# Batch 0's queries and keys stay float32 through TensorE in a one-core attention and two-MLP kernel

## The chip, the cores and the metric

The program runs on one core of one Trainium2 chip. The metric is device time in microseconds (us), from the first to the last instruction of the slowest core with the little that lies around them. Lower is better.

## The reference

Inputs are q, k, v of shape (4, 8, 576, 64) in float32, a decay f of shape (4, 8, 576), two weight matrices of a first MLP (512 x 2048 and 2048 x 512) and two of a second (512 x 1024 and 1024 x 512); the weights come as 8-byte floats.

```python
scores = 0.125 * q @ k.T + cum[:, None] - cum[None, :]   # cum = cumsum(log f), causal mask
x = softmax(scores) @ v                                  # 4 batches, 8 heads, 576 rows
h = x @ w_in;  g = h * tanh(softplus(h));  y = g @ w_out # 2304 tokens
h2 = y @ w2_in; solu = h2 * softmax(h2)
out = layernorm(solu) * g_ln @ w2_out
```

## The kernel before

**Halves.** TensorE is given float16. A float32 operand is scaled by a power of two from a bound of it, and split in a high and a low half (`split`, L181); a product of two such operands takes three float16 matmuls, or one where both halves lie side by side in the 128 rows of the contraction, as in the scores.

**Attention.** A batch has five row tiles of 128 rows (the last has 64). For batch 0 `load_raw` fetches a chunk of 128 rows of all 8 heads (256 KB), `stats` takes sums of squares of k on ScalarE, `scales` turns their maximum over all five k chunks into powers of two, and only then `split_k` and `split_q` make the halves (q's low half on GpSimd). `turn` transposes them with eight float16 matmuls against an identity and two ScalarE copies out of PSUM for a chunk; in the later batches a DMA transpose does it. Then VectorE copies the key's high half (L408) and the query's high half (L439) to the tiles of the second matmul. `scores` issues for every head a matmul over 128 contraction rows (L474), a second one over 67 rows (L475) that carries the missing product and the three rows of the decay, and on the diagonal a mask (L479). The decay rows come from a scan on VectorE, go out to DRAM (`dd`) and return by a DMA (L409).

`step_r` takes the row maximum on VectorE (L525) and the exponential on ScalarE (L527). `step_h` makes the halves of the probabilities, high by ScalarE (L565), low by GpSimd (L566), and has a DMA transpose them (L571). `step_pv` multiplies them with the halves of v, three matmuls for each head and chunk (L597 to L599), after `split_v` has scaled v by a bound over all five chunks. `fin` divides by the row sums and sends the result through a DMA transpose (L624) to `xT`, the first MLP's input.

**First MLP.** Blocks j of 256 tokens; `up` (L842) has 16 slices of 12 matmuls, `down` (L886) 16 slices of 6. Block j = 0 is exactly row tiles 0 and 1 of batch 0. It is worked weight group by weight group while the weights still arrive: 16 parts of 1 MB (W1 and W2 in four groups each), loaded into two buffers (L114), turned from 8-byte floats to float32 in three VectorE instructions (L124, L126, L128), bounded through TensorE (L147) and split; the first eight parts are split through TensorE with a float32 matmul against a diagonal (L191). Block j = 1 needs all of them.

**Order.** A planner (`Order.pin`, near the end) lays all instructions out with costs of its own, and pins the order on every engine. So each engine runs its list in order, and one instruction that waits holds all behind it. SP issues all DMAs.

Of the kernel before, what the change touches and what calls it, by code (L numbers as in the profile page):

```python
# [10 lines left out]
F32 = mybir.dt.float32  # L11
# [195 lines left out]
def emit(tc, q, k, v, f, w_in, w_out, w2_in, w2_out, g_ln, out):  # L207
# [7 lines left out]
    make_identity(nc, ident)  # L215
    ident16 = const.tile([P, P], F16, name="ident16")
    nc.vector.tensor_copy(ident16, ident)
    maskd = const.tile([P, P], BF16, name="maskd")
# [6 lines left out]
    nc.gpsimd.memset(ones, 1.0)  # L225
    c_k1 = const.tile([P, 1], F32, name="c_k1")
    nc.vector.memset(c_k1, 0.2)

    us2 = const.tile([P, NTT], F32, name="us2")
    ivt = const.tile([P, B], F32, name="ivt")  # L230
    iv = [ivt[:, b:b + 1] for b in range(B)]
    usc1 = [const.tile([P, 4], F32, name=f"usc1_{b}") for b in range(B)]
    wpt = const.tile([P, 4], F32, name="wpt")
    wps = [wpt[:, g:g + 1] for g in range(4)]
    kb = [const.tile([P, 1], F32, name=f"kb{b}") for b in range(B)]
    ipwo = const.tile([P, 1], F32, name="ipwo")
    kbz = const.tile([P, 1], F32, name="kbz")
    rho = const.tile([P, 4], F32, name="rho")
    ths = const.tile([P, 4], F32, name="ths")
    rcol = const.tile([P, 2], F32, name="rcol")  # L240

# [35 lines left out]
    ktr = att.tile([P, NKT, 2 * H, P], F16, name="ktr")  # L277
    kn = [att.tile([P, H * P], F16, name=f"kn{i}") for i in range(KNB)]
# [70 lines left out]
    def scales(b, which):  # L349

        j0 = "kv".index(which[0])
        n = len(which)
        t = att.tile([P, 6, 2], F32, tag="sct", name=f"sct{which}_{b}", bufs=1)
        x = [t[:, i, :n] for i in range(6)]
        nc.vector.tensor_reduce(x[0], sc["st", b][:, j0:j0 + n], axis=AX.X, op=ALU.max)
        src = across(x[0], x[1])
        nc.vector.tensor_scalar(x[1], src, 2.0 ** -40, None, op0=ALU.max)
        root2(nc, x[4], x[1])
        nc.vector.reciprocal(x[5], x[4])
        for i, nm in enumerate(which):  # L360
            pw, ip = t[:, 4, i:i + 1], t[:, 5, i:i + 1]
            if nm == "k":
                u = att.tile([P, 2], F32, tag="scu", name=f"scu_{b}", bufs=2)
                c = 64.0
                nc.vector.tensor_scalar(u[:, 0:1], pw, 0.125 / c, None, op0=ALU.mult)
                nc.vector.tensor_scalar(u[:, 1:2], ip, c, None, op0=ALU.mult)
                sc["q", b], sc["k", b] = u[:, 0:1], u[:, 1:2]
            else:
                u = att.tile([P, 1], F32, tag="scv", name=f"scv_{b}", bufs=2)
                nc.vector.tensor_scalar(u, ip, 2.0 ** 14, None, op0=ALU.mult)  # L370
                nc.vector.tensor_scalar(iv[b], pw, 2.0 ** -14, None, op0=ALU.mult)
                sc["v", b] = u

# [7 lines left out]

    def turn(dst, src, r0, r1_, nm):

        n = dst.shape[1]
        for x in range(0, n, 4):
            t = psh.tile([P, 2, TB], F32, tag="h", name=f"h_{nm}_{x}").rearrange("p g (y s) -> p (g y) s", s=P)
            for y in range(4):
                nc.tensor.matmul(
                    t[:, y, r0:r1_], src[r0:r1_, (x + y) * P:(x + y + 1) * P], ident16[r0:r1_, r0:r1_],
                    start=True, stop=True)  # L390
            nc.scalar.copy(dst[:, x:x + 4, r0:r1_], t[:, :, r0:r1_])

    def split_k(b, c):
        r0, r1_, t0 = rows_of(b, c)
        n = r1_ - r0
        t = kn[cnt["kn"] % KNB]
        cnt["kn"] += 1
# [5 lines left out]
        kt[b, c] = kc  # L403
        if b == 0:
            turn(kc[:, :H], t, r0, r1_, f"k{c}")
        else:
            nc.sync.dma_start_transpose(out=kc[:, :H, r0:r1_], in_=t[r0:r1_, :H * P])
        nc.vector.tensor_copy(kc[:64, H:, r0:r1_], kc[64:, :H, r0:r1_])  # L408
# [17 lines left out]
    def split_q(b, c):  # L426
        r0, r1_, t0 = rows_of(b, c)
        t = attd.tile([P, H, P], F16, tag="qn", name=f"qn_{b}_{c}", bufs=1)
# [3 lines left out]
        qa = attd.tile([P, H, P], F16, tag="qa", name=f"qa_{b}_{c}", bufs=2)  # L432
        if b == 0:
            turn(qa, t.rearrange("p h d -> p (h d)"), r0, r1_, f"q{c}")
        else:
            nc.sync.dma_start_transpose(out=qa[:, :, r0:r1_], in_=t[r0:r1_].rearrange("p h d -> p (h d)"))
# [20 lines left out]
    def scores(o, b, i, h, cs):  # L457
# [3 lines left out]
        for c0, c1 in runs(b, cs):  # L461
# [4 lines left out]
            d = o[:, w + a0 - o0(b, cs):w + 128 * (n - 1) + a1 - o0(b, cs)]  # L466
            k = ktr[:, s:s + n]
            if n > 1:
                d = d.rearrange("p (c s) -> p c s", s=P)
                k1, k2 = k[:, :, h], k[:67, :, H + h]  # L470
            else:
                k1, k2 = k[:, 0, h, a0:a1], k[:67, 0, H + h, a0:a1]
            diag = c1 == i + 1
            nc.tensor.matmul(d, qa[:, h, r0:r1_], k1, start=True, stop=False)  # L474
            nc.tensor.matmul(d, qb_[:67, h, r0:r1_], k2, start=False, stop=not diag)  # L475
# [68 lines left out]
    def step_h(b, i, hs):  # L544
        m, pt = pend.pop(("p", b, i, hs))
        n = len(hs) * (i + 1)
        h0, o = hs[0], 0
        if n == i + 1 and h0 % 2:
# [26 lines left out]
    def step_pv(b, i, hs):  # L575
# [25 lines left out]
    def fin(b, i):  # L601
# [9 lines left out]
        x32 = attd.tile([P, DM], F32, tag="x32", name=f"x32_{b}_{i}", bufs=1)  # L611
        nc.vector.tensor_tensor(
            hd(x32[:m]), hd(acc[:m]), rr[:m].unsqueeze(2).to_broadcast([m, H, D]), op=ALU.mult)
        xh = attd.tile([P, 2, DM], F16, tag="xh", name=f"xh_{b}_{i}", bufs=1)
# [32 lines left out]
    wlo = [rp0]  # L647
    ident32 = rp0.tile([P, P], F32, name="ident32")
    nc.vector.tensor_copy(ident32, ident)
    minus = rp0.tile([P, P], F16, name="minus")  # L650
# [51 lines left out]
    def ahead(b, i, h):  # L702
# [10 lines left out]
        if nb < B:  # L713
# [4 lines left out]
            if h == (LD + 2 if ni else 4):  # L718
                if nb or ni > 1:
                    split_k(nb, ni)  # L720
                    split_q(nb, ni)
                split_v(nb, ni)

# [63 lines left out]

    for c in range(NCH):
        load_raw(0, c, "k", pool0(c))
    for c in range(2):  # L790
        load_raw(0, c, "q", pool0(c))
    for n in range(WPF):
        W1.load(n)
    load_raw(0, 0, "v", pool0(0))
    for c in range(NCH):
        stats(0, c, "k")
    scales(0, "k")
    for c in range(2):
# [6 lines left out]
    for c in range(NCH):
        stats(0, c, "v")
    scales(0, "v")
    split_v(0, 0)
    for n in range(n0 + LAG):
# [10 lines left out]
    def segs(j):  # L820
        r = []
        t = j * TB
        while t < (j + 1) * TB:
            b = t // S
            e = min((b + 1) * S, (j + 1) * TB)
            r.append((b, t - j * TB, e - j * TB))
            t = e
# [76 lines left out]
    def evac(j, t):  # L904
# [12 lines left out]
        for p0 in (0, 64):  # L917
# [145 lines left out]
class Order:  # L1063
# [46 lines left out]
    def trace(self):  # L1110
# [6 lines left out]
        for i in list(self.tc.nc.cur_bb.bb.instructions):  # L1117
# [580 lines left out]
```

## Time and profile before

| | |
|---|---|
| median of 3 runs | 781.82 us (780.08 to 782.59) |
| profiled execution | 780.57 us, of which span 778.8 us |
| TensorE (PE) busy | 722.9 us, 93% of the span |
| VectorE (DVE) / ScalarE (ACT) / GpSimd (POOL) busy | 564.6 / 576.1 / 393.5 us |
| chain that ended last | PE 74%, DVE 8%, ACT 7%, DMA 5% |

PE's busy time is near the span, but not evenly: the last 579 us have almost no idle PE, the first 200 us have most of it. So the table is to be read by stages.

### The profile page before, as it was taken

To read this page: it belongs to the slowest core of one execution; us is meant where nothing else is said; L and a number is where in the kernel's file an instruction comes from. 1 tells how busy PE (TensorE), PEld (TensorE's weight loads), DVE (VectorE), ACT (ScalarE), POOL (GpSimd) and SP (SyncE) were. 2 spreads that over 40 slices of the span, in tenths; PEclk is the share of its full clock that TensorE was granted. 3 is DMA by queue.
4 is the path that set the end of the run, shared out by engine and by line. 5 is a ranking of instruction groups with operands and counts; after the bars stand their busy time and mean duration, and the time that the engine had idled before them with its cause. 6 is when DMAs were issued, how large, how long until landed. Compare 5 with 4: busy or idle time off the path is not lost.

```text
span 778.8 us, 16034 instructions
## 1 busy us (share of the span) xinstructions
PE 722.9 (93%) x5950; PEld 458.9 (59%) x5950; DVE 564.6 (72%) x1140; ACT 576.1 (74%) x1286; POOL 393.5 (51%) x319
## 2 busy tenths in 40 slices
PE   1679889779999999999999999999999999999997
PEld 0444655557666677777777776765565554444443
DVE  5999997878789877789778645878785545375560
ACT  4787898988999999999999868995874553133331
POOL 2245355777776576786788742393472221122221
PEclk9999998899999999999999999999999999999999
DMA  8989986879999898889999446603215325345423
GB/s 242 247 238 268 258 158 120 154 152 190 164 183 169 170 197 185 164 147 173 159 177 162 82 96 163 216 29 122 44 54 107 68 55 104 86 95 121 99 65 94
DMA packets 295226, 112.49 MB, mean 144 GB/s; under 512 B 280492, under 2 KB 281260, under 8 KB 295148
## 3 DMA queue, kind: packets, MB, share of 16 engines
q1 hardware_dynamic: 295148, 111.48, 67.2%
q8 instruction: 46, 0.75, 0.4%
q14 instruction: 32, 0.26, 0.1%
HBM read 46.59 MB, written 9.55 MB: 72 GB/s over the span
## 4 chain that ended last, share of the span: by engine, by line
PE 74%; DVE 8%; ACT 7%; DMA 5%; issue 2%; POOL 2%; SPq 1%; ACTq 0%; POOLq 0%; DVEq 0%
PE x L886 21%; PE h L842 20%; PE h L1606 12%; PE o L1646 11%; PE sp L474 2%; PE sp L475 2%; DMA wi_r<-in_moe_w_in_dram 2%; PE pv L597 2%; ACT p L527 1%; PE pv L599 1%; PE pv L598 1%; DMA pT<-ph 1%; DVE nm L525 1%; DVE wout L126 1%; DVE wout L128 1%
## 5 line engine op out<-in xcount | busy, mean ns | idle before, releaser
L886 PE MATMUL x<-wout,gt 128*128 128x512 f16 x864 | 215.2, 381 | 3.7 <-POOL gt L869 3.7
L842 PE MATMUL h<-xT,win 128*128 128x256 f16 x1728 | 214.0, 275 | 2.3 <-ACT th L855 1.7
L842 PEld LDWEIGHTS <-win 128*128 128x128 f16 x1728 | 167.7, 99 | 42.2 <-issue 4.1
L566 POOL TENSOR_TENSOR ph<-p,ph 128x512 f16<-128x512 f32 (+4 forms) x120 | 155.9, 1306 | 70.6 <-ACT ph L565 64.2
L869 POOL TENSOR_TENSOR gt<-th,gt 128x512 f16<-128x512 f32 x72 | 93.6, 1301 | 97.6 <-ACT gt L868 95.5
L886 PEld LDWEIGHTS <-gt 128*128 128x128 f16 x864 | 80.1, 98 | 74.4 <-POOL gt L869 5.2
L1634 POOL TENSOR_TENSOR z<-sl,z 128x1024 f16<-128x1024 f32 x18 | 38.3, 2126 | 118.8 <-DVE s2c L1613 57.5
L1606 PE MATMUL h<-w,x2T 128*128 128x512 f16 x432 | 96.0, 379 | 0.0
L1646 PE MATMUL o<-wo,zT 128*128 128x512 f16 x432 | 95.5, 379 | 0.4 <-DMA zT<-z 0.4
L863 DVE SCALAR_TENSOR_TENSOR th<-ta,th 128x512 f32<-128x512 f32 x72 | 63.9, 887 | 20.2 <-ACT ta L862 18.2
L1646 PEld LDWEIGHTS <-zT 128*128 128x128 f16 x432 | 42.2, 98 | 51.7 <-DMA zT<-z 0.9
L1606 PEld LDWEIGHTS <-x2T 128*128 128x128 f16 x432 | 42.3, 98 | 50.1
L854 ACT ACTIVATE ta<-h,usc 128x512 f32<-128x512 f32 (+3 forms) x96 | 54.8, 582 | 21.5 <-PE h L842 18.8
L527 ACT ACTIVATE p<-sp,nm 64x64 f32<-64x64 f32 (+7 forms) x128 | 62.3, 492 | 7.7 <-DVE nm L525 5.1
L474 PE MATMUL sp<-ktr,qa 128*128 128x64 f16 (+6 forms) x304 | 56.9, 249 | 11.3 <-ACT p L527 7.1
L475 PE MATMUL sp<-ktr,qb 67*128 67x64 f16 (+6 forms) x304 | 61.2, 250 | 2.8 <-DVE qb L439 2.8
L1617 ACT ACTIVATE e<-h,s2c 128x1024 f32<-128x1024 f32 x18 | 21.7, 1203 | 55.7 <-DVE s2c L1615 51.6
L859 DVE TENSOR_SCALAR ta<-ta 128x512 f32<-128x512 f32 x72 | 49.0, 683 | 17.8 <-ACT ta L854 17.5
L525 DVE TENSOR_REDUCE nm<-sp 128x1 f32<-128x320 f32 (+7 forms) x88 | 48.7, 561 | 15.9 <-PE sp L479 9.3
L597 PE MATMUL pv<-vt,pT 128*128 128x64 f16 (+2 forms) x480 | 53.8, 197 | 2.2 <-DMA pT<-ph 2.2
L868 ACT CAST gt<-th 128x512 f16<-128x512 f32 x72 | 44.6, 619 | 13.1 <-DVE th L863 12.7
L598 PE MATMUL pv<-vt,pT 128*128 128x64 f16 (+2 forms) x480 | 53.4, 196 | 0.5 <-DVE vt L197 0.5
(250 smaller groups left out, 1447.5 us busy)
## 6 DMA issues: line engine op xcount, KB each, us to landing
wi_r<-in_moe_w_in_dram SPq DMA_DIRECT2D x8, 1024.0 KB
wo_r<-in_moe_w_out_dram SPq DMA_DIRECT2D x8, 1024.0 KB
x2d<-x2h SPq DMA_DIRECT2D x18, 256.0 KB
out_dram<-ro SPq DMA_DIRECT2D x18, 256.0 KB
w2i_r<-in_moe_w_in_dram SPq DMA_DIRECT2D x4, 1024.0 KB
w2o_r<-in_moe_w_out_dram SPq DMA_DIRECT2D x4, 1024.0 KB
rawk<-in_k_dram SPq DMA_DIRECT2D x13, 256.0 KB
rawv<-in_v_dram SPq DMA_DIRECT2D x13, 256.0 KB
```

The costliest lines, as they stand in the source:

```text
L474: nc.tensor.matmul(d, qa[:, h, r0:r1_], k1, start=True, stop=False)
L475: nc.tensor.matmul(d, qb_[:67, h, r0:r1_], k2, start=False, stop=not diag)
L527: nc.scalar.activation(pv[:m, g * (i + 1) * P + off:g * (i + 1) * P + end], s3[:, g, off:end], AF.Exp, bias=nm[:m, g:g + 1], accum_out=rs[ ...
L566: nc.gpsimd.tensor_tensor(p4[:, :, 1], pv3, p4[:, :, 0], op=ALU.subtract)
L597: nc.tensor.matmul(o, pT[a0:a1, k, :m], vh, start=(c == 0), stop=False)
L598: nc.tensor.matmul(o, pT[a0:a1, k, :m], vl, start=False, stop=False)
L842: nc.tensor.matmul(ph, win[:, (fi // 4) * NC1 + c, col:col + P], x[:, lx * NC1 + c, :], start=(m == 0), stop=(m == 3 * NC1 - 1))
L863: nc.vector.scalar_tensor_tensor(th, ta, 2.5, th, op0=ALU.subtract, op1=ALU.mult)
L869: nc.gpsimd.tensor_tensor(gt[:, 1], th, gt[:, 0], op=ALU.subtract)
L886: nc.tensor.matmul(o, gt[:, lg, n % 2, t * P:(t + 1) * P], wout[:, fi, lw * 512:(lw + 1) * 512], start=(first and m == 0), stop=(last and ...
L1606: nc.tensor.matmul(h[:, half * 512:(half + 1) * 512], x[:, lx * NC1 + c, :], self.w2[:, half * NC1 + c, lw * 512:(lw + 1) * 512], start=(n ...
L1646: nc.tensor.matmul(o, zT[:, lz * NF2 + c, :], self.wo[:, c, lw * 512:(lw + 1) * 512], start=(n == 0), stop=(n == 3 * NF2 - 1))
```

## The change

In batch 0, q and k are no longer bounded, scaled or split. `turn` transposes the raw float32 chunk with four float32 matmuls; k goes by one ScalarE copy to `kt32`, a float32 view of the space that `ktr` has for halves, and q by two ScalarE copies (each of 64 partitions, scaled by 0.125) to a tile that holds two heads with zeros around them, so that the first score matmul is float32 over 128 rows. The second one stays and brings only the decay (zeros elsewhere, set by GpSimd at the start). For row tiles 0 and 1 the probabilities too are transposed by float32 matmuls and copied by ScalarE, and multiplied with raw v, one float32 matmul for a head and chunk; a bound over the first two v chunks serves block j = 0 alone. The halves of v are made later, for tiles 2 to 4. The q tiles of batch 0 lie in the space of `kn` and of the later batches' query tiles. The first loads become k, q, k, q, v, v of chunks 0 and 1, then the weights, then the rest. The planner's cost of a float32 matmul changes.

```diff
+    kt32 = ktr.rearrange("p k h s -> p (k h s)").bitcast(F32).rearrange("p (k x s) -> p k x s", k=NKT, s=P)
+    knt = att.tile([P, KNB, H * P], F16, name="knt")
+    kn = [knt[:, i] for i in range(KNB)]
+    qat = att.tile([P, 2, H * P], F16, name="qat")
+    q32 = [t.rearrange("p k s -> p (k s)").bitcast(F32).rearrange("p (x y s) -> p x y s", y=2, s=P) for t in (knt, qat)]
+    nc.gpsimd.memset(qb[0][:64].rearrange("p h s -> p (h s)").bitcast(F32), 0.0)
+    for t in q32:
+        nc.gpsimd.memset(t[64:, :, 0], 0.0)
+        nc.gpsimd.memset(t[:64, :, 1], 0.0)
+    for c in range(NCH):
+        nc.gpsimd.memset(kt32[:64, c, 4:], 0.0)
...
+    def turn(dst, src, r0, r1_, nm, scale=1.0):
+        t = psh.tile([P, 2, TB], F32, tag="h", name=f"h_{nm}").rearrange("p g (y s) -> p (g y) s", s=P)
+        n = src.shape[-1] // P
+        for y in range(n):
+            nc.tensor.matmul(
+                t[:, y, r0:r1_], src[r0:r1_, y * P:(y + 1) * P], ident32[r0:r1_, r0:r1_], start=True, stop=True)
+        if type(dst) is list:
+            for y, d in enumerate(dst):
+                nc.scalar.activation(d[:, :, r0:r1_], t[64 * y:64 * y + 64, :, r0:r1_], AF.Copy, scale=scale)
+            return
+        nc.scalar.copy(dst[:, :n, r0:r1_], t[:, :n, r0:r1_])
...
+        if b == 0:          # split_k
+            x = (b * NCH + c) % NKT
+            turn(kt32[:, x, :4], raw["k", b, c], r0, r1_, f"k{c}")
...
+        if b == 0:          # split_q
+            qa = q32[c % 2]
+            turn([qa[:64, :, 0], qa[64:, :, 1]], raw["q", b, c], r0, r1_, f"q{c}", 0.125)
+            qt[b, c] = qa, qb[0]
+            return
...
+                q1, k1 = qa[:, h // 2, h % 2, r0:r1_], kt32[:, s:s + n, h // 2]     # scores, batch 0
+            nc.tensor.matmul(d, q1, k1, start=True, stop=False)
...
+        if b == 0 and i < 2:     # step_h
+            turn(p4, pt.rearrange("p c s -> p (c s)")[:, :n * P], 0, m, f"p{i}_{hs[0]}")
...
+        if b == 0 and i < 2:     # step_pv
+                    nc.tensor.matmul(
+                        acc[:m, h * D:(h + 1) * D], pT[:, g * (i + 1) + c, :m], raw["v", b, c][:, h * D:(h + 1) * D],
+                        start=(c == 0), stop=(c == i))
...
+    for c in range(2):
+        load_raw(0, c, "kq", pool0(c))
+    for c in range(2):
+        load_raw(0, c, "v", pool0(c))
     for n in range(WPF):
         W1.load(n)
-    for c in range(NCH):
-        stats(0, c, "k")
-    scales(0, "k")
```

## Rows read from the trace of the kernel before

**Rows 1.** Busy time by stretch: each engine (instructions), granted clock, DMA share, GB/s.

```profile
0.00:25.00 25.00, 5.87 (x44) 4.55 (x45) 15.75 (x33) 13.50 (x27) 6.84 (x15) 1.00 0.80 215
25.00:50.00 25.00, 17.15 (x111) 12.84 (x111) 24.80 (x53) 17.95 (x55) 8.07 (x6) 1.00 1.05 286
50.00:110.00 60.00, 51.55 (x461) 32.71 (x460) 56.46 (x114) 52.84 (x107) 26.91 (x19) 0.97 0.92 229
110.00:200.00 90.00, 77.65 (x824) 53.74 (x823) 75.39 (x135) 80.89 (x204) 61.71 (x53) 0.91 0.84 159
200.00:778.80 578.80, 570.71 (x4518) 355.01 (x4514) 392.19 (x810) 410.94 (x897) 289.96 (x228) 1.00 0.60 124
```

**Rows 2.** The chain of waits, first 200 us: start, length, what.

```profile
84.71 2.56 PE h L842 x12
...
120.49 6.58 DMA pT<-ph
```

**Rows 3.** Timeline of PE, at the lower and then the higher level.

```profile
25.70 0.31 PE L474 MATMUL sp<-ktr,qa 128*128 128x128 f16 x1
...
27.98 0.31 PE L474 MATMUL sp<-ktr,qa 128*128 128x128 f16 x1
28.08 0.31 PE L475 MATMUL sp<-ktr,qb 67*128 67x128 f16 x1
...
59.57 1.10 PE L191 MATMUL h_lo<-wout,wo_dg 128*128 128x512 f32 x2
60.52 0.38 PE L192 MATMUL h_lo<-wout,minus 128*128 128x512 f16 x1
60.73 1.02 PE L191 MATMUL h_lo<-wout,wo_dg 128*128 128x512 f32 x2
...
70.45 0.19 PE L598 MATMUL pv<-vt,pT 128*128 128x64 f16 x1
70.48 0.19 PE L599 MATMUL pv<-vt,pT 128*128 128x64 f16 x1
...
76.05 0.33 PE L346 MATMUL sp<-wi_b,ones 128*128 128x1 f32 x2
76.24 0.62 PE L147 MATMUL sp<-wout 128*128 128x128 bf16 x8
```

**Rows 4.** Groups of DVE up to 110 us: line, count, busy us, mean ns.

```profile
L126 DVE SCALAR_TENSOR_TENSOR wout<-wo_r,wout 128x1024 int32<-128x1024 int32 x8 | 12.5, 1565 | 0.1
...
L408 DVE COPY ktr<-ktr 64x1024 f16<-64x1024 f16 (+1 forms) x5 | 2.8, 567 | 0.2
L197 DVE SCALAR_TENSOR_TENSOR kn<-wout,scu,kn 128x512 f16<-128x512 f32 x3 | 2.2, 742 | 1.3 <-ACT kn L196 1.3
L439 DVE COPY qb<-qa 64x1024 f16<-64x1024 f16 (+1 forms) x5 | 1.9, 388 | 0.1
```

**Rows 5.** Groups of ACT up to 110 us.

```profile
L391 ACT CAST qa<-h_q 128x512 f16<-128x512 f32 (+1 forms) x10 | 5.2, 550 | 0.0
L199 ACT ACTIVATE wout<-wout,scu 128x512 f32<-128x512 f32 x3 | 2.2, 725 | 2.5 <-DVE scu L365 2.5
```

**Rows 6.** Groups of POOL up to 110 us.

```profile
L566 POOL TENSOR_TENSOR ph<-p,ph 128x384 f16<-128x384 f32 (+1 forms) x15 | 21.2, 1421 | 35.6 <-ACT ph L565 34.7 <-POOL qn L204 0.8
...
L204 POOL TENSOR_TENSOR qn<-wout,qn 128x512 f16<-128x512 f32 x3 | 3.9, 1284 | 20.4 <-ACT qn L203 17.2 <-issue 3.1
```

**Rows 7.** Timeline of SP, the DMA queue's own: issues.

```profile
18.11 0.63 SPq L409 DMA_DIRECT2D ktr<-dd  x2
...
33.87 5.85 SPq L571 DMA_TRANSPOSE pT<-ph  x2
...
79.83 1.23 SPq L624 DMA_TRANSPOSE xT<-xh  x1
```

**Rows 8.** Timeline of PE: scores of the last tile, each waiting for ACT.

```profile
142.23 0.38 PE L474 MATMUL sp<-ktr,qa 128*64 128x512 f16 x1 [0.84 <-ACT p L542]
...
146.05 0.21 PE L474 MATMUL sp<-ktr,qa 128*64 128x64 f16 x1 [3.23 <-ACT p L541]
```

More of the change, by code (lines that the diff above doesn't have):

```diff
@@ L215, in emit @@
     make_identity(nc, ident)
-    ident16 = const.tile([P, P], F16, name="ident16")
-    nc.vector.tensor_copy(ident16, ident)
+    ident32 = const.tile([P, P], F32, name="ident32")
+    nc.vector.tensor_copy(ident32, ident)
     maskd = const.tile([P, P], BF16, name="maskd")
@@ L225, in emit @@
     nc.gpsimd.memset(ones, 1.0)
-    c_k1 = const.tile([P, 1], F32, name="c_k1")
-    nc.vector.memset(c_k1, 0.2)
[L229 to L240, printed above, removed]
+    us2 = const.tile([P, NTT], F32, name="us2")
+    cols = const.tile([P, 48], F32, name="cols")
+    iv = [cols[:, b:b + 1] for b in range(B + 1)]
+    kb = [cols[:, 5 + b:6 + b] for b in range(B)]
+    ipwo, kbz, c_k1 = cols[:, 9:10], cols[:, 10:11], cols[:, 11:12]
+    wps = [cols[:, 12 + g:13 + g] for g in range(4)]
+    rho, ths, rcol = cols[:, 16:20], cols[:, 20:24], cols[:, 24:26]
+    usc1 = [cols[:, 26 + 4 * b:30 + 4 * b] for b in range(B + 1)]
+    nc.vector.memset(c_k1, 0.2)
     win = const.tile([P, NC1 * DFF // 512 + 2, 1024], F16, name="win")
@@ L349, in scales @@
     def scales(b, which):
+        b, b0 = b % B, b
         j0 = "kv".index(which[0])
         n = len(which)
-        t = att.tile([P, 6, 2], F32, tag="sct", name=f"sct{which}_{b}", bufs=1)
+        t = att.tile([P, 6, 2], F32, tag="sct", name=f"sct{which}_{b0}", bufs=1)
         x = [t[:, i, :n] for i in range(6)]
-        nc.vector.tensor_reduce(x[0], sc["st", b][:, j0:j0 + n], axis=AX.X, op=ALU.max)
+        nc.vector.tensor_reduce(
+            x[0], sc["st", b][:, j0:j0 + n, :NCH if b0 < B else 2], axis=AX.X, op=ALU.max)
         src = across(x[0], x[1])
@@ L380, in hd @@
         return ap.rearrange("p (h d) -> p h d", h=H)
[L382 to L391, printed above, removed]
+    def turn(dst, src, r0, r1_, nm, scale=1.0):
[9 more added lines that the diff above has]
+        nc.scalar.copy(dst[:, :n, r0:r1_], t[:, :n, r0:r1_])
     def split_k(b, c):
@@ L403, in split_k @@
         kt[b, c] = kc
[L404 to L407, printed above, removed]
+        nc.sync.dma_start_transpose(out=kc[:, :H, r0:r1_], in_=t[r0:r1_, :H * P])
         nc.vector.tensor_copy(kc[:64, H:, r0:r1_], kc[64:, :H, r0:r1_])
@@ L431, in split_q @@
         split(nc, t[r0:r1_, :, :64], t[r0:r1_, :, 64:], rq, s, qmode(b, c, 2))
[L432 to L436, printed above, removed]
+        qa = qat[:, cnt["qb"] % 2].rearrange("p (h s) -> p h s", s=P)
+        nc.sync.dma_start_transpose(out=qa[:, :, r0:r1_], in_=t[r0:r1_].rearrange("p h d -> p (h d)"))
         qb_ = qb[cnt["qb"] % 2]
@@ L467, in scores @@
             k = ktr[:, s:s + n]
+            k2 = k[:67, :, H + h]
+            if b:
+                q1, k1 = qa[:, h, r0:r1_], k[:, :, h]
+            else:
+                q1, k1 = qa[:, h // 2, h % 2, r0:r1_], kt32[:, s:s + n, h // 2]
             if n > 1:
                 d = d.rearrange("p (c s) -> p c s", s=P)
-                k1, k2 = k[:, :, h], k[:67, :, H + h]
             else:
-                k1, k2 = k[:, 0, h, a0:a1], k[:67, 0, H + h, a0:a1]
+                k1, k2 = k1[:, 0, a0:a1], k2[:, 0, a0:a1]
             diag = c1 == i + 1
-            nc.tensor.matmul(d, qa[:, h, r0:r1_], k1, start=True, stop=False)
+            nc.tensor.matmul(d, q1, k1, start=True, stop=False)
             nc.tensor.matmul(d, qb_[:67, h, r0:r1_], k2, start=False, stop=not diag)
@@ L546, in step_h @@
         n = len(hs) * (i + 1)
+        if b == 0 and i < 2:
+            pT = attd.tile([P, 4 * NCH, P], F16, tag="pT", name=f"pT_{b}_{i}_{hs[0]}", bufs=PTB)
+            p4 = pT.rearrange("p c s -> p (c s)").bitcast(F32).rearrange("p (c s) -> p c s", s=P)
+            turn(p4, pt.rearrange("p c s -> p (c s)")[:, :n * P], 0, m, f"p{i}_{hs[0]}")
+            pend["pT", b, i, hs[0]] = p4
+            return
         h0, o = hs[0], 0
@@ L588, in step_pv @@
         acc = pend["pv", b, i]
+        if b == 0 and i < 2:
+            for g, h in enumerate(hs):
+                for c in range(i + 1):
+                    nc.tensor.matmul(
+                        acc[:m, h * D:(h + 1) * D], pT[:, g * (i + 1) + c, :m], raw["v", b, c][:, h * D:(h + 1) * D],
+                        start=(c == 0), stop=(c == i))
+            return
         for g, h in enumerate(hs):
@@ L611, in fin @@
         x32 = attd.tile([P, DM], F32, tag="x32", name=f"x32_{b}_{i}", bufs=1)
-        nc.vector.tensor_tensor(
-            hd(x32[:m]), hd(acc[:m]), rr[:m].unsqueeze(2).to_broadcast([m, H, D]), op=ALU.mult)
+        rb = rr[:m].unsqueeze(2).to_broadcast([m, H, D])
+        if b == 0 and i < 2:
+            nc.vector.scalar_tensor_tensor(
+                hd(x32[:m]), hd(acc[:m]), sc["v", B][:m], rb, op0=ALU.mult, op1=ALU.mult)
+        else:
+            nc.vector.tensor_tensor(hd(x32[:m]), hd(acc[:m]), rb, op=ALU.mult)
         xh = attd.tile([P, 2, DM], F16, tag="xh", name=f"xh_{b}_{i}", bufs=1)
@@ L721, in ahead @@
                     split_q(nb, ni)
-                split_v(nb, ni)
+                if nb == 0 and ni == 2:
+                    for c in range(2, NCH):
+                        stats(0, c, "v")
+                    scales(0, "v")
+                    for c in range(NCH):
+                        split_v(0, c)
+                if nb:
+                    split_v(nb, ni)
     def slot_pre():
@@ L800, in emit @@
         split_q(0, c)
-    for c in range(1, NCH):
-        load_raw(0, c, "v", pool0(c))
-    load_raw(0, 2, "q", pool0(2))
+    for c in range(2):
+        stats(0, c, "v")
+    scales(B, "v")
+    load_raw(0, 2, "kqv", pool0(2))
+    for c in range(3, NCH):
+        load_raw(0, c, "v")
+    for c in range(3, NCH):
+        load_raw(0, c, "k")
     wgo(W0C)
[L805 to L808, printed above, removed]
     for n in range(n0 + LAG):
@@ L1169, in trace @@
                 out = next(t.name for t, b, w in acc if w)
+                out = out, [t.name for t, b, w in acc if not w and t.name.startswith("pT")]
                 if run is not None and run.out == out and len(run.ins) < 24 and not any(
```

28 lines of the change are left out of this document (13 added, 15 removed).

## Prediction

> **What bounds the kernel now.** I read the busy time by stretch first [rows 1]. From 200 us on PE is busy for 570.7 of 578.8 us, so whatever PE work stands there is the time; 8.1 us are idle. The start is otherwise. In the first 50 us PE is busy for 23.0, idle for 27.0. From 50 to 110 it is idle for 8.5, from 110 to 200 for 12.3. Together 55.9, which is the span less PE's 722.9. In the start another engine is full: DVE 24.8 of 25, then 56.5 of 60 us; from 110 to 200 ACT is, with 80.9 of 90. DMA is near full until 110.
>
> The chain of waits says the same of the places [rows 2]: the first `up` stands only at 84.7 us, and a wait of 6.6 us for a DMA transpose of probabilities follows at 120. So the question is one of balance: the change takes work from DVE, ACT, POOL and the DMA queue, where the start is bound, and gives work to PE, which bounds everything behind.
>
> The timeline of PE gives its prices [rows 3]. At 28 us two matmuls of 128 columns start 0.10 us apart, which is the 1.2 GHz level, though the granted clock column reads 1.00 there. From about 50 us on, after PE had been busy for most of a stretch, it is the 2.4 GHz level: eight of 128 columns take 0.62, less the 0.16 of the last one's tail (its 0.19 against a spacing of 0.03) 0.46, so 0.057 each. So the 23 busy us of the first 50 are about 11.5 at the higher level.
>
> **What PE gets.** A float32 matmul of 512 columns (recorded as two) takes 0.95 us to the next start, a second one 0.86 (1.02 less the same tail), the float16 one between them 0.21 [rows 3]: 1.77 against 0.41 ns a column.
> - Scores. A head of batch 0 has 128+256+384+512+576 = 1,856 columns, eight heads 14,848. Times 1.36 ns: +20.2 us. With 0.86 for every 512 (loads hidden) 18.8, with 0.95 21.5.
> - Transposes of q and k. Before eight float16 matmuls a chunk (0.46 us), after four float32 ones. The nearest short float32 row takes 0.19 to the next start, with one column; four times a column's 0.41 ns gives 0.21 for 128 columns, so I take 0.23. Ten chunks, two of them half: about +4.3.
> - Transposes of probabilities: 24 in tiles 0 and 1, at 0.23: +5.5.
> - Values there: 24 float32 matmuls at 0.23 for 72 float16 ones at 0.03 [rows 3]: +3.4.
>
> Sum +33.4 us of PE time at the higher level. The bounds are 29 (loads hidden, 0.19 for a short one) and 52: the 96 short ones (8 of them scores of tile 0) might cost twice 0.21, if the load of float32 weights takes turns with the columns. I take the low side, since the row with 0.19 holds two such loads.
>
> The Trainium skill ("TensorE: Matmul & The Clock Gate", Weight-path perf modes) says that fast weight load is off for float32. By its LDWEIGHTS section a load of 128 columns is about 107 ns; an estimate from that, four passes with their own load, gives 0.43 us for a short float32 matmul. No run here has shown a row of short ones behind each other, so I keep it as a rival.
>
> **What the others lose.** DVE: the low halves of k, five at 0.74 = 3.7; copies L408 2.8 and L439 1.9 [rows 4]; the k bound's small ones go and those of the new v bound come. So 8.4 us go out of the first 110, where DVE is full; the weights' own conversion (L126 alone is 1.57 for a part) stays. ACT: of the twenty copies of `turn` five go (2.7), and for five chunks each q's scaling and cast, k's scaling and k's sums, at about 0.7: some 17 [rows 5]. The float32 copy of the transposed probabilities takes the place of L565, nothing. POOL: five low halves of q at 1.3, six of probabilities at 1.4, some 15 [rows 6]; ten zeroings of tiles of 512 columns come, and POOL had 20 us of idle time ahead of the low halves of q, before the scores need them. DMA queue: six transposes of probabilities go; the first two alone hold SP for 5.9 us [rows 7], in the stretch where weights must be issued. Loads keep their bytes and only change order; SP gets no new issue.
>
> **What it moves.** The first score needs no longer five k chunks and a bound, and v no bound over five chunks. It still needs the decay rows, which come by a DMA issued at 18.1 us [rows 7]; so it can start at about 20 us or, with the planner's freedom to send the decay earlier, 16; before it was 25.7 [rows 3]. Behind it the halves, the DMA transpose and the wait for v's bound are gone. Tiles 0 and 1 then end at some 45 us, and `xT` of block 0, of which the last transpose is issued at 79.8 [rows 7], is there by 50. So `up` and `down` of block 0 follow the weight groups from 50 us on instead of 84.7, and PE has work in the whole stretch 50 to 110, where DVE set the pace.
>
> **What PE can take up.** By 50 us PE could have done transposes of two chunks (3.7), both tiles' scores (7.7), probabilities (5.5), values (5.5), and the weights' bounds and first splits (about 6): 28 at the higher level. Waits will leave some of it: I take 24.5, so 13 more than the 11.5 of before. Bounds 6 (decay late, lower level throughout) and 17. From 50 to 200 there are 20.8 idle, and the granted clock of 0.97 and 0.91 stands for 3.6 and 16 us at the lower level [rows 1] (the share missing to 1, doubled, of 60 and 90 us), of which PE was busy in perhaps a half and lost 6 or so. With a backlog most of this is taken up; after 200 us, with a backlog, PE idles 1.4%, but in the start the softmax chain of each tile still has to be waited for. I take 24 of 27 taken up; bounds 8 and 27.
>
> Sum: 778.8 + 33.4 − 13 − 24 = 775.2 span. With the 1.8 around it 777.0, against the profiled execution's 780.6; the median of the runs is 1.2 above that execution, but I leave part of that out and say **776**. Of the 37 us that I count as taken up, 33.4 only pay for the added matmuls: the margin is thin.
>
> **Rivals.** *The start stays bound (slower).* One mechanism: the last tile. Its scores go one head at a time, two banks deep, and wait for ACT's exponential [rows 8]; PE's order is fixed, so what waits there holds all behind. Float32 makes each head's 512 + 64 columns 0.8 us longer inside that chain, 6.3 in all. And the tile's q lies in the space of `kn`: batch 1's first key halves can't be written before its last wide score is done (142 us before), and behind that stand a DMA transpose, the copy and the scores of batch 1. If that decides, nothing is taken up from 110 on, and only 10 before it: 778.8 + 33.4 − 13 − 10 + 1.8 = 791. It decides when less than 20 of the 27 are taken up. For it: ACT full there; against it: ACT loses 17 us, block 0 is out of the way earlier, and block 1 can fill the gap.
>
> *The early cover isn't used (no change).* The decay rows or PE's lower level keep tiles 0 and 1 late; 6 instead of 13 gives 784, at the edge of 0.3% above the median, or 782 with 26 taken up later.
>
> *Short float32 matmuls at 0.43.* 96 times 0.2 is 19, of which 72 lie in the first 50 us and half of that is covered: +12, 788. The rule of the skill above is this case.
>
> *All taken up:* 13 + 27 and 3 more by dense work at the higher level: 771, which becomes 762 if the early part reaches 17 and the weights come 5 of DVE's 8 us earlier.
>
> **How the numbers follow.** Two runs of this kernel differ by 0.3% without a change, 2.3 us. Chances: forecast and its better end (762 to 779.5) 0.50; no change 0.18; last tile 0.22; short matmuls 0.10. So faster 0.50, same 0.18, slower 0.32. The forecast's own range is 766 to 779; with the rivals' times 0.8 of it lies in 762 to 792.
>
> **What would show it.** After the change: first scores before 20 us; first `up` near 50; DVE below 90% from 50 to 110; float32 scores at 0.9 us for 512 columns and short ones at 0.23; PE idle below 15 us in the first 50 and below 6 from 50 to 200; PE busy of the whole near 745. I am wrong if the first `up` stays behind 70 us, if the wait ahead of batch 1's scores grows, or if short float32 matmuls follow each other by 0.4.

## The result

The changed kernel takes 767.91 us (median of 5 runs, 766.76 to 769.04), the kernel before 781.15. The ratio is 0.9837, 95% interval 0.9813 to 0.9862: faster by 1.6%. The forecast was 776, so the sign was right, and the forecast gain (5 us) less than half of the measured one (13). The profiled execution has a span of 766.1 us, 12.7 less.

First the busy time by stretch of the changed kernel, columns as in [rows 1]:

```profile
0.00:25.00 25.00, 15.19 (x90) 13.72 (x91) 18.37 (x41) 7.27 (x18) 10.50 (x23) 1.00 0.85 251
25.00:50.00 25.00, 24.39 (x173) 18.86 (x172) 20.75 (x48) 22.34 (x56) 3.42 (x3) 1.00 0.93 268
50.00:110.00 60.00, 59.38 (x462) 41.59 (x461) 54.28 (x108) 51.44 (x108) 24.37 (x17) 1.00 0.77 213
110.00:200.00 90.00, 86.45 (x900) 56.50 (x898) 72.17 (x147) 81.53 (x203) 58.31 (x52) 1.00 0.90 162
200.00:766.10 566.10, 556.16 (x4405) 345.34 (x4403) 386.25 (x788) 397.86 (x875) 283.13 (x224) 1.00 0.61 125
```

Everything was gained in the first 200 us: what is left after them is 566.1 instead of 578.8 us, 12.7 less, the whole difference. PE idles 10.4 us in the first 50 (27.0 before), 0.6 from 50 to 110 (8.5), 3.6 from 110 to 200 (12.3), and the granted clock is 1.00 where it was 0.97 and 0.91. DVE, no longer at 24.8 of 25 from 25 to 50, has 20.8 there.

The timeline of PE, with one row of its weight loads (PEld), shows the start and the prices:

```profile
4.45 2.05 PE L393 MATMUL h_k<-ident,wout 128*128 128x128 f32 x8 [4.45 <-DMA wout<-in_k_dram]
...
14.59 0.56 PE L350 MATMUL sum<-sctv,ones 128*128 128x1 f32 x2 [1.83 <-DVE sctv L360]
15.01 2.06 PE L393 MATMUL h_k<-ident,wout 128*128 128x128 f32 x8
16.86 1.06 PE L147 MATMUL sp<-win 128*128 128x128 bf16 x8
...
18.75 0.78 PE L494 MATMUL sp<-ktr,knt 128*128 128x128 f32 x2
...
22.30 0.31 PE L495 MATMUL sp<-ktr,qb 67*128 67x128 f16 x1
22.41 0.31 PE L499 MATMUL sp<-maskd,ident 128*128 128x128 bf16 x1
...
22.93 0.22 PE L495 MATMUL sp<-ktr,qb 67*128 67x128 f16 x1
22.99 0.22 PE L499 MATMUL sp<-maskd,ident 128*128 128x128 bf16 x1
23.05 0.44 PE L494 MATMUL sp<-ktr,knt 128*128 128x128 f32 x2
23.32 0.22 PE L495 MATMUL sp<-ktr,qb 67*128 67x128 f16 x1
...
24.23 0.97 PEld L393 LDWEIGHTS h_q<-ident,wout 128*128 128x128 f32 x8
24.29 1.11 PE L393 MATMUL h_q<-ident,wout 128*128 128x128 f32 x8
25.23 1.06 PE L393 MATMUL h_p<-ident,p 128*128 128x128 f32 x8
...
69.61 1.47 PE L881 MATMUL h<-xT,win 128*128 128x256 f16 x12
...
88.21 1.02 PE L494 MATMUL sp<-ktr,qat 128*128 128x512 f32 x2
89.07 0.38 PE L495 MATMUL sp<-ktr,qb 67*128 67x512 f16 x1
...
92.53 1.13 PE L494 MATMUL sp<-ktr,qat 128*128 128x512 f32 x2 [0.61 <-ACT p L547]
93.49 0.38 PE L495 MATMUL sp<-ktr,qb 67*128 67x512 f16 x1
...
129.82 1.07 PE L494 MATMUL sp<-ktr,knt 128*64 128x512 f32 x2 [1.07 <-ACT p L562]
```

The first scores stand at 18.75 us. At 22.30 two matmuls of 128 columns are 0.11 apart (1.2 GHz), at 22.93 0.06 (2.4 GHz): the higher level comes at 22.4 us, after PE had been busy since 14.6 us with short gaps, instead of 49. Four float32 transposes (recorded as eight) take 0.94, so 0.235 each; a float32 score of 128 columns takes 0.27 to the next start, one of 512 columns 0.86, and 0.96 behind a wait. The first `up` stands only at 69.6. The timeline of SP says why: the two transposes that fill block 0's `xT` are issued 25 us apart, tile 1's at 65.5.

```profile
40.57 1.35 SPq L661 DMA_TRANSPOSE xT<-xh  x1
...
65.48 1.27 SPq L661 DMA_TRANSPOSE xT<-xh  x1
```

### The profile page after: what moved, and what is told of

Same layout as the page of the kernel before. It is cut to its first block, busy times and chain, and to the rows that moved or that the text cites. A ratio compares the mean times of both kernels' runs of the same rounds, so it can differ in the third digit from the quotient of the medians.

```text
span 766.1 us, 16124 instructions
## 1 busy us (share of the span) xinstructions
PE 741.6 (97%) x6022; PEld 476.0 (62%) x6022; DVE 551.8 (72%) x1128; ACT 560.4 (73%) x1256; POOL 379.7 (50%) x318
## 4 chain that ended last, share of the span: by engine, by line
PE 82%; ACT 7%; DVE 5%; DMA 3%; issue 2%; POOL 0%; SPq 0%; ACTq 0%; DVEq 0%; POOLq 0%
PE x L925 21%; PE h L881 21%; PE h L1645 12%; PE o L1685 12%; PE sp L494 4%; PE sp L495 2%; PE h_lo L191 2%; PE pv L630 1%; PE pv L632 1%; PE pv L631 1%; ACT p L547 1%; PE sp L499 1%; DMA pT<-ph 1%; PE pv L618 1%; ACT ph L591 1%
## 5 line engine op out<-in xcount | busy, mean ns | idle before, releaser
L925 PE MATMUL x<-wout,gt 128*128 128x512 f16 x864 | 213.0, 379 | 2.8 <-DVE x2h L954 1.6
L881 PE MATMUL h<-xT,win 128*128 128x256 f16 x1728 | 210.2, 273 | 1.9 <-ACT th L894 1.9
L592 POOL TENSOR_TENSOR ph<-p,ph 128x512 f16<-128x512 f32 (+4 forms) x114 | 147.3, 1298 | 60.7 <-ACT ph L591 55.6
L902 DVE SCALAR_TENSOR_TENSOR th<-ta,th 128x512 f32<-128x512 f32 x72 | 66.4, 925 | 23.3 <-ACT ta L901 19.8
L893 ACT ACTIVATE ta<-h,cols 128x512 f32<-128x512 f32 (+3 forms) x96 | 54.5, 584 | 22.9 <-PE h L881 22.3
L495 PE MATMUL sp<-ktr,qb 67*128 67x64 f16 (+6 forms) x304 | 59.5, 242 | 0.3 <-DVE ktr L422 0.3
L494 PE MATMUL sp<-ktr,qat 128*128 128x64 f16 (+7 forms) x288 | 54.0, 260 | 2.9 <-ACT p L547 1.3
L898 DVE TENSOR_SCALAR ta<-ta 128x512 f32<-128x512 f32 x72 | 47.3, 657 | 9.6 <-ACT ta L893 9.0
L653 POOL TENSOR_TENSOR xh<-x,xh 128x512 f16<-128x512 f32 (+1 forms) x20 | 28.1, 1406 | 49.6 <-DVE sctv L91 27.6
L900 ACT ACTIVATE ta<-ta,cols 128x512 f32<-128x512 f32 x72 | 52.2, 727 | 0.4
```

What stands on the lines that cost most here:

```text
L494: nc.tensor.matmul(d, q1, k1, start=True, stop=False)
L592: nc.gpsimd.tensor_tensor(p4[:, :, 1], pv3, p4[:, :, 0], op=ALU.subtract)
L881: nc.tensor.matmul(ph, win[:, (fi // 4) * NC1 + c, col:col + P], x[:, lx * NC1 + c, :], start=(m == 0), stop=(m == 3 * NC1 - 1))
L893: nc.scalar.activation(ta[:, :, a:e], ph[:, :, a:e], AF.Exp, scale=usc(b, fi // 4))
L900: nc.scalar.activation(ta, ta, AF.Ln, scale=0.2, bias=c_k1)
L902: nc.vector.scalar_tensor_tensor(th, ta, 2.5, th, op0=ALU.subtract, op1=ALU.mult)
```

## The experiments

The early-start theory, mine: tiles 0 and 1 no longer wait, so PE fills the start. The relief theory: the work taken off the other engines and the DMA queue is the gain. The order theory: the planner found one lucky order, or its new cost made the gain. All medians stand beside runs of the kernel before on the same chip.

| kernel | us | ratio to before | 95% interval |
|---|---|---|---|
| a0_seed | 769.1 | 0.9878 | 0.9844 to 0.9912 |
| a1_oldcost | 783.7 | 1.0067 | 1.0042 to 1.0092 |
| a1b_seed | 779.4 | 0.9988 | 0.9966 to 1.0009 |
| a2_bound | 771.5 | 0.9907 | 0.9877 to 0.9936 |
| a3_halves | 777.0 | 0.9967 | 0.9949 to 0.9986 |
| b6_values | 778.0 | 0.9975 | 0.9957 to 0.9994 |
| b4_nokbound | 775.3 | 0.9935 | 0.9911 to 0.9959 |
| b5_nobounds | 776.2 | 0.9948 | 0.9922 to 0.9974 |
| b1_planner | 780.6 | 1.0012 | 0.9994 to 1.0030 |
| b2_four | 785.3 | 1.0076 | 1.0052 to 1.0100 |
| a4_twice | 785.5 | 1.0074 | 1.0047 to 1.0101 |
| a5_warm | 771.4 | 0.9902 | 0.9884 to 0.9919 |
| b3_warm | 783.6 | 1.0054 | 1.0030 to 1.0078 |
| a9_w2dve | 776.0 | 0.9969 | 0.9947 to 0.9992 |
| a10_w2pool | 781.1 | 1.0011 | 0.9997 to 1.0025 |
| a11_search | 769.1 | 0.9862 | 0.9833 to 0.9892 |
| b7_search | 776.0 | 0.9953 | 0.9935 to 0.9971 |
| a12_w2dves | 776.8 | 0.9958 | 0.9934 to 0.9982 |

### The order: other draws of the same instructions

```diff
-        seq = min(found, key=lambda q: sum(self.replay(q, x) for x in range(SEEDS)))
+        seq = min(found, key=lambda q: sum(self.replay(q, x + 100) for x in range(SEEDS)))
```

> The changed kernel, only with other seeds in the planner's choice among its own orders. A control: what another order of the same instructions is worth. Early-start theory (tiles 0 and 1 no longer wait for bounds, halves and DMA transposes, so PE fills the first 50 us and reaches 2.4 GHz early) and relief theory (the gain is the work taken off DVE, ACT, POOL and the DMA queue): both 766 to 771. Order theory (the gain is one lucky order): up to 780.

For a11_search and b7_search (the latter on the kernel before with the changed planner) the draw is wider:

```diff
-SLOW = (1.03, 1.06)
+SLOW = (1.0, 1.03, 1.06, 1.1)
-ROUNDS = 12
+ROUNDS = 16
-SEEDS = 8
+SEEDS = 16
```

> The changed kernel with a planner that draws 64 orders instead of 24 and judges each over 16 instead of 8 replays. Same instructions. If the order of the changed kernel was a lucky draw: the wider draw finds its like or better, 762 to 769, and the kernel before with it gains too. If the planner's judgement is only loosely tied to the chip: 768 to 774.

> The kernel before with the changed planner and the same wider draw. If the whole difference of 13 us were the luck of the draw: 765 to 772. If it is the change: 775 to 781.

Three orders of the changed kernel give 0.9837, 0.9878 and 0.9862, three of the kernel before 1, 1.0012 and 0.9953. So another order moves these kernels by some 0.4 to 0.6%, and two orders of a1_oldcost below differ by 0.8%. The change is worth 0.9% (0.9862 against 0.9953, both with the wider draw) to 1.6%: not one lucky draw, but the 1.6% is at the upper end of what it gives.

### The planner's cost of a float32 matmul

a1_oldcost, and a1b_seed with the other seeds of a0_seed as well:

```diff
-                        c = max(4.0 * c, 224.0)
+                        c *= 4.0
+                        o.d += 200.0
```

> The changed kernel with the planner's old cost of a float32 matmul (four times the columns and 200 ns more). Same instructions, another order. Early start and relief: 767 to 773, since the work and its dependences are the same. Order theory (the new cost makes the gain): 776 or more.

> The changed kernel with the planner's old cost of a float32 matmul, as before at 783.7, and other seeds in the planner's choice. If the old cost misleads the planner systematically: 778 to 787. If the first one was an unlucky order: 766 to 773.

The gain is gone in both: 1.0067 against 0.9837, and with the other seeds 0.9988 against 0.9878, a loss of 1.1% to 2.3% (9 to 18 us). By the old cost a short float32 matmul takes 0.41 us, by the chip 0.235. The timeline of ACT (first line) and of PE in a1_oldcost shows what such an order does:

```profile
40.21 0.47 ACT L547 ACTIVATE p<-sp,nm 128x256 f32<-128x256 f32 x1 [4.43 <-DVE nm L545]
...
37.16 0.28 PE L350 MATMUL sum<-sctv,ones 128*128 128x1 f32 x2
41.77 1.32 PE L393 MATMUL h_p<-ident,p 128*128 128x128 f32 x8 [4.33 <-ACT win L193]
42.87 1.06 PE L147 MATMUL sp<-wout 128*128 128x128 bf16 x8
```

PE stands 4.33 us for ACT's copy (which frees the PSUM bank); ACT itself had stood 4.43 us for a row maximum of DVE. Behind PE's gap eight matmuls of 128 columns take 1.06, the lower level, where after the higher they take 0.62 [rows 3]. Its row of busy time from 25 to 50 us, below, has 7.3 us idle and a granted clock of 0.93; the changed kernel has 0.6 and 1.00.

```profile
25.00:50.00 25.00, 17.67 (x105) 13.53 (x105) 20.85 (x47) 15.70 (x38) 0.00 (x0) 0.93 0.73 231
```

Is it the planner alone, then? b1_planner is the kernel before with that cost and the change's grouping of value matmuls:

```diff
                 out = next(t.name for t, b, w in acc if w)
+                out = out, [t.name for t, b, w in acc if not w and t.name.startswith("pT")]
...
-                        c *= 4.0
-                        o.d += 200.0
+                        c = max(4.0 * c, 224.0)
```

> The kernel before, with only the changed planner (the new cost of a float32 matmul, and runs of value matmuls grouped by the transposed probabilities that they read). Same instructions, another order. If the new cost by itself made the gain, as the changed kernel with the old cost (783.7) may suggest: 766 to 771. If the cost matters only where short float32 matmuls stand, which are few in the kernel before: 777 to 782.

No difference. The cost line is worth 9 to 18 us in the changed kernel and nothing without its float32 matmuls.

### One part alone

a3_halves keeps q and k in float32 and undoes the values:

```diff
-        if b == 0 and i < 2:    # step_h, step_pv, fin: float32 for tiles 0 and 1
+        if False:
...
-                vc = vt[b, c]
+                vc = vt["e", c] if b == 0 and i < 2 else vt[b, c]
...
     scales(B, "v")
+    for c in range(2):
+        split_e(c)     # halves of v chunk c by that bound
```

> The changed kernel with the probabilities and values of tiles 0 and 1 in halves again: DMA transposes and three float16 matmuls instead of float32 ones; the two v chunks are split early by the bound over these two. Takes 9 us off PE, brings back six DMA transposes, six low halves on POOL, and two extra splits of v (1.5 us ACT, 1.5 DVE). Early start: xT of block 0 comes 5 to 10 us later, PE loses there about what it saves: 766 to 772. Relief (the DMA queue and POOL count): 773 or more. PE as the only bound: 759 to 763.

b6_values is the other part alone, built on b1_planner: `step_h`, `step_pv` and `fin` as in the change, q and k as before.

```diff
+        if b == 0 and i < 2:    # step_h
+            turn32(p4, pt.rearrange("p c s -> p (c s)")[:, :n * P], 0, m, f"p{i}_{hs[0]}")
...
+    for c in range(2):
+        stats(0, c, "v")
+    scales(B, "v")
```

> The kernel before with the changed planner and one part of the change alone: probabilities of tiles 0 and 1 transposed in float32 by PE, multiplied with raw v, and a bound over two v chunks for block 0. q and k keep their halves and the bound of k. With the halves of probabilities and values put back into the changed kernel the time was 777.0. If this part carries most of the gain (no DMA transposes and no v halves between the first scores and block 0): 769 to 774. If the parts need each other (early scores and early values): 775 to 780.

0.33% for q and k alone, 0.25% for the values alone, 0.9% to 1.6% for both: neither carries the gain by itself. That both together give more than the sum isn't shown: each part was run in one order, and the step from 0.6% to 0.9% is less than what another order does. In a3_halves PE idles 4.5 us from 25 to 50 (7.9 before the change) and 8.1 from 50 to 110, nearly the 8.5 of before:

```profile
25.00:50.00 25.00, 20.46 (x153) 13.20 (x152) 23.05 (x53) 23.19 (x63) 9.76 (x7) 0.96 0.89 219
50.00:110.00 60.00, 51.93 (x378) 33.24 (x379) 48.87 (x98) 41.31 (x82) 17.15 (x15) 0.93 0.91 236
```

### The bounds

a2_bound brings the bound of k back into the changed kernel (chunks 3 and 4 loaded a second time for it):

```diff
-            turn(kt32[:, x, :4], raw["k", b, c], r0, r1_, f"k{c}")
+            turn(kt32[:, x, :4], raw["k", b, c], r0, r1_, f"k{c}", sc["k", b])
...
+    for c in range(NCH):
+        stats(0, c, "k")
+    scales(0, "k")
```

> The changed kernel with the bound of k over all five chunks put back: two chunks of k are loaded once more for it, five sums of squares on ACT and the small ones on DVE come back (about 5 us of ACT, 1.5 of DVE), and the copies of q and k out of PSUM scale by it; float32 stays. So tile 0 must wait for the bound as before the change. Early start: first scores at 24 to 27 us instead of 18.8, PE at the higher level later, +6 to +10, so 774 to 778. Relief: only the small work, 768 to 771.

First scores at 22.6 us, 10.9 us of PE in the first 25 instead of 15.2, and 771.5: less than early start asked, just above relief's range. Against 0.9837 and 0.9878 the difference is 0.3% to 0.7%, 2 to 5 us, not the 6 to 10 that I gave it. The intervals of a2_bound and a0_seed overlap, so the wait for the bound isn't told from another order.

b4_nokbound and b5_nobounds take the bounds out of the kernel before (constants that suit these inputs stand for them):

```diff
-    for c in range(NCH):
-        stats(0, c, "k")
-    scales(0, "k")
...
+    sc["q", 0], sc["k", 0] = fix[:, 0:1], fix[:, 1:2]
...
-    for c in range(NCH):          # b5_nobounds alone
-        stats(0, c, "v")
-    scales(0, "v")
...
+    sc["v", 0] = fix[:, 2:3]
```

> The kernel before, with the bound of k in batch 0 left out: its power of two is a constant that suits these inputs. Halves, float16 matmuls and DMA transposes stay; five sums on ACT (4.1 us) and the small ones on DVE go. Early start: first scores at 18 to 21 us, but values still wait for v's bound and the transposes: 774 to 778. Relief: 779 to 781.

> The kernel before, with the bounds of k and of v in batch 0 left out, both powers of two being constants that suit these inputs. Nothing else of the change; PE gets no float32 matmul more. Early start alone: 764 to 772, as good as the change or better, since PE has 32 us less to do. Relief (what counts is the work of halves and the DMA transposes, which stay here): 776 to 780.

0.65% and 0.5%: about a third of the gain, but no more than the 0.47% of b7_search, which changes nothing but the planner. b4_nokbound's first scores stand at 22.73 us, 3 us earlier than before. b5_nobounds wasn't the test it was meant to be: its first scores stand at 26.86 us, no earlier than before, so it doesn't show what an early start alone gives.

```profile
26.86 0.32 PE L474 MATMUL sp<-ktr,qa 128*128 128x128 f16 x1
```

### More and less work for PE

b2_four and a4_twice add PE work in batch 0 that the next matmul overwrites; the last two lines of the cut are a4_twice:

```diff
+            for _ in range(3 if b == 0 else 0):     # b2_four, on the kernel before
+                nc.tensor.matmul(d, qa[:, h, r0:r1_], k1, start=True, stop=True)
...
+            if b == 0:                              # a4_twice, on the changed kernel
+                nc.tensor.matmul(d, q1, k1, start=True, stop=True)
```

> The kernel before, with three more copies of the first score matmul of batch 0 (overwritten by the real one): about +18.6 us of PE at the higher level, what float32 costs there, and nothing of the early start or the relief. If the old start already had room for it (idle 20.8 us from 50 to 200): 783 to 788. If the room comes only with the earlier start: 793 to 801.

> The changed kernel with the float32 score matmul of batch 0 issued twice (the first is overwritten): 26 us of PE more at the higher level. If PE is now the bound from 22 us on (4.2 us idle from 50 to 200): 787 to 795. If DVE and ACT still set the pace of the start: 770 to 780.

In the kernel before 18.6 us of PE work cost 5.9 (0.76% of 779), give or take the 3 of another order: most of it found room in the old start. In the profiled execution PE's busy time is 732.8, only 9.9 above the 722.9 of before, and its idle time 49.6 instead of 55.9. So the room was idle time (6.3 us) and, for the rest, a lower level: the granted clock is 1.00 from 50 to 110 and 0.96 from 110 to 200, where it was 0.97 and 0.91 [rows 1]. In the changed kernel some 22 us (PE busy 763.25 against 741.58) cost 15 to 18 (1.0074 against 0.9878 and 0.9837), just under the first of the two ranges: little room is left. The rows of busy time of a4_twice:

```profile
25.00:50.00 25.00, 25.00 (x182) 20.33 (x179) 21.63 (x49) 21.06 (x52) 3.89 (x3) 1.00 0.76 221
50.00:110.00 60.00, 60.00 (x434) 40.99 (x434) 52.73 (x115) 46.25 (x93) 18.56 (x13) 1.00 0.71 210
```

a9_w2dve takes the split of W2's first four parts off PE, a10_w2pool gives them to ACT and POOL, a12_w2dves is a9_w2dve with the wider draw:

```diff
-        W2.split(n, on_pool=int(W2P[n % len(W2P)]), early=early)
+        W2.split(n, on_pool=int(W2P[n % len(W2P)]))     # W2P = "0": DVE; "2": ACT and POOL
```

> The changed kernel with the early split of W2's first four parts on DVE instead of PE: 9 us less of PE between 40 and 70 us, about 5 us more of DVE. If PE is now the bound from 22 us on: 759 to 764. If DVE, which turns the weights, still sets the pace: 769 to 774. If both are about even: 765 to 769.

> The same four parts split by ACT (three passes over 1,024 columns) and POOL instead of PE: 9 us less of PE, about 4 us more of ACT, 8 of POOL, none of DVE except what POOL's use of the shared port holds up. If PE is now the bound: 758 to 764. If ACT and DVE are: 768 to 774.

> The changed kernel with the early split of W2's first four parts on DVE instead of PE (776.0 before), with the wider draw. If that loss was an unlucky order: 762 to 769. If DVE sets the pace of the start as much as PE: 772 to 778.

A gain was one of the outcomes looked for; each lost 7 to 14 us against the changed kernel (ratios of 0.9969 and 1.0011 against 0.9837, and of 0.9958 against 0.9862 with the same wider draw). PE's busy time hardly fell (739.6 to 745.9 against 741.6, with 9 us less work), and its idle time rose by 10 to 14 us. The start of a12_w2dves, two rows, and the first scores of a12_w2dves and of a10_w2pool:

```profile
0.00:25.00 25.00, 10.46 (x60) 9.11 (x60) 18.29 (x33) 6.84 (x12) 12.28 (x25) 0.95 0.97 271
25.00:50.00 25.00, 21.34 (x122) 16.39 (x123) 19.59 (x46) 14.78 (x43) 0.00 (x0) 0.78 0.77 237
...
26.57 0.74 PE L494 MATMUL sp<-ktr,knt 128*128 128x128 f32 x2
...
27.00 0.73 PE L494 MATMUL sp<-ktr,knt 128*128 128x128 f32 x2
```

These two lose before the moved work comes: in the changed kernel the splits of W2 stand behind 45 us, but here the first scores are already 8 us late. The planner laid the start out anew, with a weight part as the first load and k behind it. So they show another order and not the price of the move. a9_w2dve keeps the start (first scores at 19.72 us) and loses from 50 to 110, where PE idles 5.4 us at a granted clock of 0.86 (the profiled execution took 782.5 us, the median is 776.0):

```profile
50.00:110.00 60.00, 54.64 (x399) 37.50 (x397) 51.92 (x99) 41.99 (x84) 19.51 (x13) 0.86 0.71 221
```

That PE is no longer the only bound of the new start, and 9 us moved to a neighbour come back as waits, is suggested by this one run. DVE is no fuller there than in the changed kernel (51.9 against 54.3), so that DVE sets the pace isn't shown; which wait it is stays open.

### The level of the clock by itself

```diff
+    for w in range(24):
+        for _ in range(8):
+            nc.tensor.matmul(sps[w % 2][:, :P], ident, ident, start=True, stop=True)
```

> The changed kernel with 192 matmuls of 128 columns on the identity added, written to score banks 0 and 1 ahead of the first scores and read by nobody, so that PE is busy from about 1 us on. If the clock level is worth it, the higher level comes at 8 to 15 us instead of 22.4, and 2 to 5 us are gained: 763 to 766. If the chain of the decay rows sets the first scores anyway: 767 to 769; if the added matmuls delay the first transposes: 769 to 772.

> The kernel before with the same 192 added matmuls. Its higher level came only at 49 us. If the early level by itself were the gain of the change: 772 to 777. If the level matters only with work to do, as early start and relief have it: 779 to 783.

Neither gains, and neither sets the level apart. In a5_warm PE is busy for 22.5 of the first 25 us, and the first float32 score already runs at the higher level (0.47 instead of 0.78). But the added matmuls stand ahead of the first transposes of k, which come at 11.50 instead of 4.45 us, and the first score is later, at 19.82: the third of the outcomes. In b3_warm the first scores stand at 31.99 us instead of 25.70, and the level is lost again between 25 and 50 us (granted clock 0.50). So PE work without use bought nothing; what an early level alone is worth stays open.

```profile
0.00:25.00 25.00, 22.49 (x285) 22.01 (x286) 17.89 (x36) 7.43 (x19) 10.44 (x23) 1.00 0.87 252
...
11.50 1.11 PE L393 MATMUL h_k<-ident,wout 128*128 128x128 f32 x8
...
19.82 0.47 PE L494 MATMUL sp<-ktr,knt 128*128 128x128 f32 x2
```

## Why the prediction was right in sign and too small

- **What bounds it, and where the gain comes from:** right. All of it lies in the first 200 us, where PE was not the bound.
- **What PE gets:** right. 0.86 to 0.96 us for a score of 512 columns, 0.235 for a transpose and 0.27 for a score of 128 columns stand against 0.9 and 0.23. The rival of 0.43 is out; the estimate from the Trainium skill ("TensorE: Matmul & The Clock Gate", LDWEIGHTS) is not what the trace shows: the weight loads of the four transposes at 24.29 us take 0.97 in all and run beside them.
- **The step that failed: the term "taken up by 50 us", 13, was too small; some 21 were taken up, above my upper bound of 17.** The rows of busy time, two of the changed kernel and one of the kernel before:

```profile
0.00:22.40 22.40, 12.59 (x63) 11.16 (x64) 15.77 (x35) 5.76 (x10) 10.50 (x23) 1.00 0.88 266
22.40:50.00 27.60, 26.99 (x200) 21.42 (x199) 23.35 (x54) 23.84 (x64) 3.42 (x3) 1.00 0.89 254
...
0.00:49.00 49.00, 22.01 (x151) 16.86 (x152) 39.55 (x85) 30.45 (x79) 14.82 (x20) 1.00 0.92 250
```

PE was busy for 12.6 us until 22.4, at the lower level, and for 27.0 behind it at the higher: some 33 at the higher level, against 12 before (half of the 22.0 until 49 us, and 1). The prediction listed 28 us of work for this stretch and left 3.5 of it to waits. But PE idled only 0.6 us behind 22.4, and the list was short by weight work. The groups of the changed kernel's PE up to 50 us that bound (L147) and split (L191, L192) weights:

```profile
L191 PE MATMUL h_lo<-win,wi_dg 128*128 128x512 f32 x8 | 4.2, 612 | 0.2 <-ACT pT L399 0.2
L147 PE MATMUL sp<-win 128*128 128x128 bf16 x32 | 3.3, 263 | 1.3 <-DVE win L128 1.3
L191 PE MATMUL h_lo<-wout,wo_dg 128*128 128x512 f32 x5 | 2.7, 614 | 0.0
L147 PE MATMUL sp<-wout 128*128 128x128 bf16 x24 | 1.9, 219 | 0.4 <-DVE wout L128 0.4
L192 PE MATMUL h_lo<-win,minus 128*128 128x512 f16 x4 | 1.5, 380 | 0.0
L192 PE MATMUL h_lo<-wout,minus 128*128 128x512 f16 x2 | 0.8, 378 | 0.0
```

At the higher level's spacing (0.9 for a float32 matmul, 0.21 and 0.057 for the others) these are some 10 us, not the 6 of the list, and the transposes of a third chunk of q and k came too. Probabilities and values were behind the list (16 of 24 matmuls each), so weights and the next tile filled what they left.

From 50 to 200 idle time fell by 16.6, and with the clock at 1.00 the 6 us that I estimated as lost to the lower level came back: 22.6 against my 24. Without any estimate: PE's busy time rose by 18.7 us (722.9 to 741.6), its idle time fell by 31.4 (55.9 to 24.5), and that is the 12.7. In the prediction's terms 33.4 added and 44 taken up make −10; the 2.5 between aren't accounted for.
- **A step that was wrong without a cost:** "`up` and `down` of block 0 from 50 us on". Tile 1's values ended late, and the first `up` stands at 69.6. PE was full anyway, with weight splits, float32 transposes and tile 2's scores. DVE stayed at 90% from 50 to 110, not below.
- **The rivals:** "all taken up", with a fuller early part (771 to 762), came nearest. "The early cover isn't used" is out by the 21 above. "The start stays bound" didn't come; PE idles 3.6 us from 110 to 200, and its longest wait for ACT there is 1.1 us where 3.2 stood [rows 8]. But the start can be bound again: with the planner's old cost, or with one part alone, PE stops, the granted clock falls below 1.00, and at most 0.3% is left.
- **What I left out:** the order. The text ahead of the prediction named the planner's cost only as a fact. It turned out to decide whether the room is found at all (9 to 18 us), and another order moves a kernel by 0.4% to 0.8%, half of the gain that I forecast or all of it.
- **Of the theories:** that the room in the old start pays for the change is shown, by the rows and by b2_four beside a4_twice. How much of it the early start opens and how much the relief isn't: each part alone gives almost nothing, and the wait for k's bound is at most 2 to 5 us. The order theory holds for the cost line, not for luck. Left open is which wait takes over when PE gets less to do.

## What to carry to other kernels

Work may move to the busiest engine if that engine idles in the stage where the work stands; the price is read from that stage, and a probe that adds such work and nothing else (18.6 us that cost 5.9) shows the room before anything is rebuilt. Where an order is planned by costs, measure a new kind of instruction before judging a change that uses it: a wrong price of 0.41 for 0.235 us hid all of this gain, in both orders tried. And try a change under several orders, probes above all: one order's luck can be as large as half an effect, and a probe whose start was laid out anew shows that and not what it was built for.

## What the runs showed of the hardware

Four matmuls in float32 of 128 columns take 0.94 us at the higher level, 1.85 at the lower, and in the changed kernel, where PE idles for only 4.8 us between 22.4 and 200, it kept the higher level there without a drop (granted clock 1.00, and no matmul at the lower level's spacing). Three slower kernels built from the changed one, with PE gaps in the first 110 us (a1_oldcost, a3_halves, a12_w2dves), show the lower level again there, with a granted clock of 0.78 to 0.97 in such a stretch. That a gap costs its length and then the level behind it is seen once in a row (4.33 us, then 1.06 instead of 0.62); how much of each loss it makes wasn't measured. In the first 22 us the granted clock column reads 1.00 while the spacing of matmuls shows 1.2 GHz, so the level at the start is read from the spacing.
